# Block-sparse attention and a SoLU layer: where the first batch's mask factors are made, and how the weights and the first x come in

## The chip, the core and the metric

The kernel runs on one core of a Trainium2 chip. A core has five engines with an in-order queue each: TensorE (PE in the profile; PEld is its weight load), VectorE (DVE), ScalarE (ACT), GpSimd (POOL) and SyncE (SP), which here only issues DMAs. Data lie in SBUF, matmuls write to PSUM, and POOL works on SBUF alone. The metric is the device time of one execution in microseconds (us). The kernel before took 225.47 us, the median of three runs (225.02 to 226.38).

## The reference

Four batches, eight heads, 768 positions, head size 64. Positions are in 24 blocks of 32. A query block sees its neighbours, the first and the last block, three sampled key blocks, and the first and last query blocks see all. Then comes a layer of two weight matrices with SoLU (h times its softmax) and a layer norm with a gain between them.

```python
scores = scale * np.matmul(q, k.transpose(0, 1, 3, 2))
mask = np.abs(blk_i - blk_j) <= 1
mask = mask | (blk_i == 0) | (blk_j == 0) | (blk_i == 23) | (blk_j == 23)
for qb in range(24):
    for kb in sampled_blocks[qb]:
        mask[qb*32:(qb+1)*32, kb*32:(kb+1)*32] = True
attn = softmax(np.where(mask, scores, -1e9))
x = np.matmul(attn, v)                      # -> (3072, 512): all heads side by side
h = x @ w_in                                # w_in 512 x 1024
solu = h * softmax(h)
ln = (solu - mean(solu)) / sqrt(var(solu) + 1e-6) * g_ln
out = ln @ w_out                            # w_out 1024 x 512
```

## The kernel before, in words

**The mask as 24 more rows.** The masked scores come out of one matmul with 88 contraction rows: 64 of the head, and 24 in which KT holds which block a key belongs to (`selT`, one row per block) and QT holds -30000 or 0 for each pair of query and key block. KT and QT are `[128, heads x 6 chunks, 128]` in bf16, two of each, for alternating batches. The 24 rows depend on neither batch nor head, so they are written once into each of the two buffers (`mask_rows`, L595, which copies 24 x 1536 for two heads at a time).

**From k and q to KT and QT.** `load` (L302) brings k, q or v of a pair of heads as fp32 (position = 6 times partition plus chunk), `cast` (L317) makes bf16 in `kn`, `qn` (two heads side by side, 128 columns) or `VA` (v with a column of ones), `turn_mm` (L326) transposes a chunk of both heads on PE into PSUM, and `turn_out` (L339) copies the two halves of 64 rows to the two heads' places. In the first batch DVE copies straight from PSUM; later DVE copies the bank once to `pt` and POOL copies the halves.

**Units.** Twelve passes (batch and two of six query chunks) have twelve slots each (four head pairs, three units of key chunks): slot s has four score matmuls (`scores`, L363, into one of two `sco` buffers of PSUM), one exponential of 128 x 1024 on ACT (`exps`, L377) and eight matmuls of 65 columns (`outs`, L385, into the one `op` bank). After a pair's third unit `normalise` (L401) divides on DVE and so frees `op`. After a pass `x_turn` (L417) transposes x with a DMA, and the following pass's slots carry its two token tiles: `h_mms` (L422, into the one `h` buffer), `e_exp`, `solu` (DVE reads `h` last), `ln_turn` (DMA), `stats` and `rstd`, `o_mms` (L482, into the one bank `o`), `scaled`, `store`. The transposes of k and q from the second batch on use the bank `o` too.

**The order is written by hand.** `at(when, fn, ...)` (L290) puts a step into a plan; `emit` sorts it by `when`, counted in slots, and every engine gets its instructions in that order. A step's `when` is therefore no time, only a place in each engine's queue. What stands before slot 0 is issued in the order of the code. `zeros` (L557) are matmuls of zeros that keep PE busy at the start.

**The weights.** w_in (fp32 in memory) comes in one DMA from the POOL queue that casts on the way (L654). w_out comes in four DMAs on SP into a buffer of its own; `prep_w` (L665) multiplies it by g on POOL, `prep_mean` takes its column mean by matmuls, and `prep_cen` (L681) subtracts that on DVE in eight instructions, so that the layer norm's mean needs no work later.

In the first pass `outs` run late by `lag` slots (L706), because v is cast after k and q.

## Time and profile before

| | |
|---|---|
| median of 3 runs | 225.47 us |
| the profiled execution itself | 226.19 us |
| its span, first to last instruction | 224.5 us |
| PE busy, mean granted clock | 208.4 us (93%), 0.99 |
| ACT, DVE, POOL busy | 175.0, 155.7, 110.5 us |
| first exponential (slot 0) starts | 7.82 us |
| exponentials of slots 4, 9, 12, 18 start | 12.43, 20.00, 24.39, 30.20 us |
| `e_exp` of the first token tiles | 34.45, 43.47, 53.26 us |

The span runs from the first to the last instruction; the execution's own time has 1.7 us more around it. From 80 to 200 us PE is busy for 97 to 99% of the time, so a microsecond that PE loses before that comes back nowhere. The stretch from 0 to 70 us holds all that the change touches. In the timeline's rows the columns are start, duration, engine, line and operation, what is written and read with shape and type, how many instructions are merged, and in brackets the idle time of the engine just before, with what ended it. A matmul's duration includes its way through the array; how fast matmuls follow one another is read from their starts.

### The profile page before, as it was taken

Reading aid. Unit: us, or ns where it says so; the run is one execution under the profiler, and the core shown is the slowest. Engines: PE = TensorE matmul, PEld = TensorE weight load, DVE = VectorE, ACT = ScalarE, POOL = GpSimd, SP = SyncE. Lnnn points to the kernel's source line nnn. Section 1 sums busy time; section 2 is a strip of 40 time slices with the busy share of each in tenths; the row PEclk is TensorE's granted clock in tenths of the full one; section 3 lists DMA queues with packets and bytes.
Section 4 is the critical chain, followed back from the end, with each engine's and each line's share of the span. In section 5 each row is a group of like instructions: output and inputs, shape, how many; then the busy total and the mean of one; then the engine's idle time right before and its main releaser. Section 6 shows DMA issues by size and latency. Waiting matters only on the chain.

```text
span 224.5 us, 5886 instructions
## 1 busy us (share of the span) xinstructions
PE 208.4 (93%) x2328; PEld 146.2 (65%) x2367; DVE 155.7 (69%) x354; ACT 175.0 (78%) x204; POOL 110.5 (49%) x152
## 2 busy tenths in 40 slices
PE   7997998889969999999999999999999999999992
PEld 2576875666737667668667766767766766666451
DVE  7894865986785756856865766777775576566782
ACT  4885888677765988986978988887898898877471
POOL 7999985437874333494862525646840000000000
PEclk9996999999999999999999999999999999999999
DMA  6999595249998239979729749659731552434404
GB/s 199 379 362 289 114 280 165 47 27 303 283 231 262 60 85 175 287 128 257 214 47 230 241 90 288 175 38 289 198 72 36 140 78 62 100 93 110 117 0 149
DMA packets 56149, 37.59 MB, mean 167 GB/s; under 512 B 38069, under 2 KB 51637, under 8 KB 56117
## 3 DMA queue, kind: packets, MB, share of 16 engines
q1 hardware_dynamic: 55172, 35.60, 61.4%
q0 software_dynamic: 528, 1.05, 2.5%
q10 hardware_dynamic: 416, 0.52, 0.7%
q8 instruction: 19, 0.31, 0.6%
q14 instruction: 14, 0.11, 0.2%
HBM read 23.07 MB, written 6.29 MB: 131 GB/s over the span
## 4 chain that ended last, share of the span: by engine, by line
PE 69%; POOL 8%; DVE 8%; DMA 7%; ACT 2%; issue 2%; SPq 0%; POOLq 0%; DVEq 0%; ACTq 0%
PE sco L370 24%; PE op L394 14%; PE h L427 13%; PE o L487 13%; DMA xT<-xb 7%; POOL VA L315 2%; PE tp_q L335 2%; DVE stats L462 2%; PE he L801 2%; DVE w_cen_sb L682 1%; PE tp_k L335 1%; ACT exs L381 1%; POOL kn L315 1%; POOL qn L315 1%; DVE xb L408 1%
## 5 line engine op out<-in xcount | busy, mean ns | idle before, releaser
L381 ACT ACTIVATE exs<-sco 128x1024 bf16<-128x1024 f32 x144 | 142.0, 1025 | 17.9 <-PE sco L370 15.1
L370 PE MATMUL sco<-QT,KT 88*128 88x256 bf16 x576 | 87.6, 274 | 2.0 <-ACT exs L381 1.2
L370 PEld LDWEIGHTS <-KT 88*128 88x128 bf16 x576 | 55.1, 97 | 33.3 <-issue 6.2
L394 PE MATMUL op<-VA,exs 128*128 128x65 bf16 x1152 | 52.7, 195 | 1.9 <-POOL qn L315 1.6
L394 PEld LDWEIGHTS <-exs 128*128 128x128 bf16 x1152 | 49.4, 98 | 5.6 <-issue 2.3
L427 PE MATMUL h<-w_in_sb,xT 128*128 128x512 bf16 x153 | 49.5, 378 | 3.6 <-DMA xT<-xb 2.7
L480 POOL TENSOR_TENSOR rstd<-vpe,mhalf 128x1 f32<-128x1 f32 x24 | 13.5, 561 | 70.9 <-DVE vpe L478 65.4
L487 PE MATMUL o<-w_cen_sb,lnT 128*128 128x512 bf16 x162 | 43.5, 379 | 2.1 <-DVE pt_q L344 1.4
L436 ACT ACTIVATE e<-h 128x1024 bf16<-128x1024 f32 x22 | 22.5, 1024 | 19.2 <-PE h L427 14.9
L462 DVE BATCH_NORM_STATS2 stats<-solu 128x6 f32<-128x512 bf16 x48 | 30.6, 680 | 0.0
L315 POOL COPY KT<-pt_k 64x768 bf16<-64x768 bf16 x24 | 20.0, 835 | 20.6 <-DVE pt_k L344 20.0
L407 DVE RECIPROCAL recip_all<-op 128x4 f32<-128x4 f32 x48 | 8.7, 181 | 30.6 <-PE op L394 30.2
L448 DVE TENSOR_TENSOR solu<-h,e 128x1024 bf16<-128x1024 f32 x22 | 26.7, 1215 | 1.2 <-ACT e L436 1.2
L487 PEld LDWEIGHTS <-lnT 128*128 128x128 bf16 x176 | 15.8, 97 | 15.0 <-issue 1.5
L315 POOL COPY QT<-pt_q 64x768 bf16<-64x768 bf16 x24 | 20.1, 836 | 6.9 <-DVE pt_q L344 5.5
L498 DVE TENSOR_SCALAR ot<-o,rstd 128x512 f32<-128x512 f32 x20 | 15.0, 750 | 11.0 <-issue 7.4
L408 DVE TENSOR_TENSOR xb<-op,recip_all 128x256 bf16<-128x256 f32 x48 | 20.4, 424 | 1.7
L427 PEld LDWEIGHTS <-xT 128*128 128x128 bf16 x176 | 15.6, 98 | 7.6 <-DMA xT<-xb 3.7
L315 POOL CAST qn<-st_q 128x768 bf16<-128x768 f32 (+2 forms) x19 | 13.4, 711 | 4.1 <-DMA st_q<-in_q_dram 3.7
L315 POOL CAST kn<-st_k 128x768 bf16<-128x768 f32 x15 | 12.8, 851 | 3.6 <-DMA st_k<-in_k_dram 2.0
L344 DVE COPY pt_q<-tp_q 128x768 bf16<-128x768 bf16 x12 | 6.7, 556 | 10.0 <-PE tp_q L335 10.0
L315 POOL CAST VA<-st_v 128x768 bf16<-128x768 f32 x13 | 11.6, 911 | 0.9 <-DMA st_v<-in_v_dram 0.6
(82 smaller groups left out, 152.1 us busy)
## 6 DMA issues: line engine op xcount, KB each, us to landing
st_v<-in_v_dram SPq DMA_DIRECT2D x16, 384.0 KB, 5.8
out_dram<-ot SPq DMA_DIRECT2D x23, 256.0 KB, 3.7
st_k<-in_k_dram SPq DMA_DIRECT2D x15, 384.0 KB, 4.8
st_q<-in_q_dram SPq DMA_DIRECT2D x12, 384.0 KB, 5.1
w_out_f<-in_moe_w_out_dram SPq DMA_DIRECT2D x4, 512.0 KB, 6.6
st_q<-in_q_dram SPq DMA_DIRECT2D x4, 256.0 KB, 6.6
w_in_sb<-in_moe_w_in_dram POOLq DMA_DIRECT2D x1, 1024.0 KB, 12.6
st_q<-in_q_dram SPq DMA_DIRECT2D x4, 128.0 KB, 3.8
```

The costliest lines, as they stand in the source:

```text
L315: eng.tensor_copy(out=o, in_=i)
L370: nc.tensor.matmul(sco[:, hh, kk * QW : (kk + 1) * QW], KT[b % 2][0:KR, h * NCH + 2 * u + kk, :], QT[b % 2][0:KR, h * NCH + PC * j : h * N ...
L381: nc.scalar.activation(out=exs_of[ps, pr][:, u].rearrange("p a b c -> p (a b c)"), in_=sco_of.pop(s).rearrange("p a b -> p (a b)"), func=A ...
L394: nc.tensor.matmul(op[:, hh, ic, :], exs[:, u, hh, kk, ic * TQ : (ic + 1) * TQ], VA[b % 2][:, 2 * pr + hh, 2 * u + kk, :], start=(u == 0 a ...
L408: nc.vector.tensor_tensor(out=xb_of[ps][:, :, 2 * pr * D : 2 * (pr + 1) * D].rearrange("p c (h d) -> p h c d", h=2), in0=op[:, :, :, 0:D], ...
L427: nc.tensor.matmul(h_of[ps, i][:, half, :], xT_of[ps][:, i * KD + c, :], w_in_sb[:, c, half * HF : (half + 1) * HF], start=(c == 0), stop= ...
L436: nc.scalar.activation(out=o, in_=h, func=ACT.Exp, scale=1.0, accum_out=esum_all[:, t : t + 1])
L448: nc.vector.tensor_mul(out=so, in0=h, in1=e)
L462: nc.vector.bn_stats(out=stat_of[ps, i][:, half, :], in_=so[:, half, :])
L480: nc.gpsimd.tensor_tensor(out=rstd_of[ps, i], in0=vpe, in1=mhalf, op=ALU.pow)
L487: nc.tensor.matmul(ops_of[ps, i], lnT_of[ps, i][:, c, :], w_cen_sb[:, c, :], start=(c == 0), stop=(c == KF - 1), skip_group_check=True)
L498: nc.vector.tensor_scalar(out=o, in0=i_, scalar1=r, scalar2=None, op0=ALU.mult)
```

## The change

In the first batch `kn` and `qn` get 88 columns per head, 64 of the head and 24 of the mask's factors, and each head's chunk is transposed by itself, so that the 24 rows arrive in KT[0] and QT[0] together with the head's. The factors in natural form are `oh` (made on POOL) for k, and `m_sb` for q, from six small matmuls; `mask_cols` copies them in, one copy for each head: two on POOL for the first pair's k, two on DVE for the first two chunks of the first pair's q, and then fourteen on POOL, twelve for q and k of the other pairs and two for the rest of the first q. The second buffers, KT[1] and QT[1], still get their rows by copies, one on POOL and seven on DVE. w_in and w_out come as sixteen uncast pieces of 128 x 512 on SP in buffers shared with the late q chunks, and POOL casts w_in. The first x is transposed on PE (`x_first`) and copied by DVE. The second batch's loads, casts and transposes, the column mean, and the first tile's `o` stand at other places in the plan.

```diff
+    kn = fix.tile([TQ, NP, NCH * 2 * KR], BF16, name="kn")
+    qn = fix.tile([TQ, NP, NCH * 2 * KR], BF16, name="qn")
...
+    def natural(b, pr, key):
+        t = (kn if key == "k" else qn)[:, pr]
+        if b == 0:
+            return t.rearrange("p (c h r) -> p c h r", h=2, r=KR)
+        return t[:, 0 : NCH * 2 * D].rearrange("p (c h r) -> p c h r", h=2, r=D)
...
-                       bufs={NCH: 7, 2: 4, 4: 4}[c1 - c0])
+                       bufs={NCH: 7, 2: 4, 4: 9}[c1 - c0])
...
+        src = natural(b, pr, key)
+        tp = bank(pool, f"tp_{key}{b}_{pr}_{c0}")
         turned[key, b, pr, c0] = tp
-
-    def turn_out(b, pr, key, engs, c0=0, c1=NCH):
+        if b == 0:
+            for hh in range(2):
+                for c in range(c0, c1):
+                    o = (tp[0:KR, hh, (c - c0) * TQ : (c - c0 + 1) * TQ] if pool in (p_h, p_sco)
+                         else tp[0:KR, hh * 512 + (c - c0) * TQ : hh * 512 + (c - c0 + 1) * TQ])
+                    nc.tensor.matmul(o, src[:, c, hh, :], ident, is_transpose=True,
+                                     start=(c == c0), stop=(c == c1 - 1))
+            return
+        for c in range(NCH):
+            nc.tensor.matmul(tp[:, c * TQ : (c + 1) * TQ],
+                             src[:, c].rearrange("p h d -> p (h d)"), ident,
+                             is_transpose=True, start=(c == 0), stop=(c == NCH - 1))
+
+    def turn_out(b, pr, key, eng, c0=0, c1=NCH):
...
+            w = (c1 - c0) * TQ
+            i = tp if len(tp.shape) == 3 else tp.rearrange("p (h x) -> p h x", h=2)
+            o = dst[0:KR].rearrange("p (h c) t -> p h (c t)", c=NCH)[
+                :, 2 * pr : 2 * pr + 2, c0 * TQ : c1 * TQ]
+            if w > 512:
+                for hh in range(2):
+                    copy(eng, o[:, hh], i[0:KR, hh, 0:w])
+            else:
+                copy(eng, o, i[0:KR, :, 0:w])
+            return
+        pt = a_sm.tile([128, S], BF16, tag="pt", name=f"pt_{key}{b}_{pr}")
+        nc.vector.tensor_copy(out=pt, in_=tp[:, 0:S])
         for hh in range(2):
             h = 2 * pr + hh
-            copy(engs[hh], dst[0:D, h * NCH + c0 : h * NCH + c1, :],
-                 tp[hh * D : (hh + 1) * D, c0 * TQ : c1 * TQ].rearrange("p (c t) -> p c t", t=TQ))
+            copy(nc.gpsimd, dst[0:D, h * NCH : (h + 1) * NCH, :],
+                 pt[hh * D : (hh + 1) * D, :].rearrange("p (c t) -> p c t", t=TQ))
...
+    def x_first(ps):
+        xT_of[ps] = mo_sb.tile([128, PC * KD, 128], BF16, tag="xT", name=f"xT{ps}")
+        tp = bank(p_o, "x_tp")
+        xb = xb_of.pop(ps).rearrange("p c m -> p (c m)")
+        for c in range(PC * KD):
+            nc.tensor.matmul(tp[:, c * 128 : (c + 1) * 128], xb[:, c * 128 : (c + 1) * 128], ident,
+                             is_transpose=True, start=(c == 0), stop=(c == PC * KD - 1))
+        nc.vector.tensor_copy(out=xT_of[ps].rearrange("p c t -> p (c t)"), in_=tp)
...
+            nc.gpsimd.affine_select(out=oh, in_=oh, compare_op=ALU.is_ge, fill=0.0,
+                                    base=base, channel_multiplier=NCH * sg,
+                                    pattern=[[sg, NCH], [-BLK * sg, NB]])
+
+        def mask_cols(eng, key, pr, m, c0=0, c1=NCH):
+            for hh in range(2):
+                copy(eng, natural(0, pr, key)[:, c0:c1, hh, D:KR], m[:, c0:c1, :])
+
+        mask_cols(nc.gpsimd, "k", 0, oh)
...
-        zeros(8)
-
+        zeros(3)
+        oh_t = bank(p_h, "oh_t")[:, 0]
+        for c in range(NCH):
+            nc.tensor.matmul(oh_t[0:NB, c * TQ : (c + 1) * TQ], oh[:, c, :], ident,
+                             is_transpose=True, start=(c == 0), stop=(c == NCH - 1))
+        selT = fix.tile([NB, NCH, TQ], BF16, name="selT")
+        zeros(3)
+
+        dist = fix.tile([NB, NB], FP32, name="dist")
+        nc.scalar.activation(out=dist, in_=io_f[:, 1], func=ACT.Square, scale=1.0)
+        nc.scalar.activation(out=seen[:, NR], in_=dist, func=ACT.Relu, scale=-0.5, bias=1.0)
+        nc.scalar.copy(out=selT.rearrange("p c t -> p (c t)"), in_=oh_t[0:NB, 0:S])
...
+        for r in range(NR):
+            nc.vector.tensor_scalar(out=seen[:, r], in0=io_f[:, 0], scalar1=samp_f[:, r : r + 1],
+                                    scalar2=None, op0=ALU.is_equal)
+        any_f = fix.tile([NB, NB], FP32, name="any_f")
+        nc.vector.reduce_max(out=any_f, in_=seen.rearrange("p r k -> p k r"), axis=AX.X)
+        mask_l = fix.tile([NB, NB], BF16, name="mask_l")
+        nc.vector.tensor_scalar(out=mask_l, in0=any_f, scalar1=0.25, scalar2=neg_r,
+                                op0=ALU.is_lt, op1=ALU.mult)
...
+        m_ps = p_sco.tile([128, 2, 512], FP32, tag="sco", name="m_ps")[:, 0, 0 : NCH * NB].rearrange(
+            "p (c r) -> p c r", c=NCH)
+        for c in range(NCH):
+            nc.tensor.matmul(m_ps[:, c, :], selT[:, c, :], mask_l, start=(c == 0),
+                             stop=(c == NCH - 1), skip_group_check=True)
+        m_sb = fix.tile([TQ, NCH, NB], BF16, name="m_sb")
+        mask_cols(nc.vector, "q", 0, m_ps, 0, 2)
+        nc.vector.tensor_copy(out=m_sb, in_=m_ps)
+        for pr in range(1, NP):
+            mask_cols(nc.gpsimd, "q", pr, m_sb)
+            mask_cols(nc.gpsimd, "k", pr, oh)
+        mask_cols(nc.gpsimd, "q", 0, m_sb, 2, NCH)
...
+        turn_out(0, 0, "k", nc.vector, 0, 2)
+        turn_mm(0, 0, "q", p_op, 0, 2)
+        turn_out(0, 0, "q", nc.scalar, 0, 2)
+        zeros(1)
+        turn_mm(0, 0, "k", p_sco, 2, NCH)
+        turn_out(0, 0, "k", nc.vector, 2, NCH)
+        zeros(1)
+        scores(0)
+        zeros(2)
+        scores(1)
+        cast(nc.gpsimd, 0, 1, "k", 0, 2, 0)
+        cast(nc.gpsimd, 0, 1, "q", 0, 2)
+        cast(nc.gpsimd, 0, 1, "k", 2, NCH, 0)
+        turn_mm(0, 1, "k", p_h, 0, 2)
+        turn_out(0, 1, "k", nc.vector, 0, 2)
+        turn_mm(0, 1, "q", p_op, 0, 2)
+        turn_out(0, 1, "q", nc.vector, 0, 2)
+        turn(0.85, 0, 1, "k", p_o, 2, NCH)
...
-            at(w0 - 1.0, mask_rows, nc.vector, KT[0], 2 * pr)
-            at(w0 - 0.99, mask_rows, nc.vector, QT[0], 2 * pr)
             turn(w0, 0, pr, "k", p_h)
             turn(w0 + (0.05 if pr == 2 else 1.0), 0, pr, "q", p_o, 0, 2)
-        for pr in range(NP):
-            at(2.0 + 0.1 * pr, cast, nc.gpsimd, 0, pr, "v")
-            at(5.0 + 0.1 * pr, cast, nc.gpsimd, 0, pr, "q", 2, NCH)
-        for pr, when in enumerate((8.9, 10.4, 12.9, 14.9)):
+        V, G = nc.vector, nc.gpsimd
+        for eng, when, t, t0, h0 in (
+            (G, 2.05, KT[1], KT[0], 0), (V, 6.9, KT[1], KT[0], 2), (V, 7.6, KT[1], KT[0], 4),
+            (V, 9.0, KT[1], KT[0], 6), (V, 16.4, QT[1], QT[0], 0), (V, 18.3, QT[1], QT[0], 2),
+            (V, 20.3, QT[1], QT[0], 4), (V, 30.4, QT[1], QT[0], 6),
+        ):
+            at(when, mask_rows, eng, t, t0, h0)
+        for n, (key, pr) in enumerate((("v", 0), ("v", 1), ("v", 2), ("q", 0), ("v", 3),
+                                       ("q", 1), ("q", 2), ("q", 3))):
+            at(2.0 + 0.1 * n, cast, nc.gpsimd, 0, pr, key, *(() if key == "v" else (2, NCH)))
+        for pr, when in enumerate((9.4, 11.9, 13.4, 15.4)):
             turn(when, 0, pr, "q", p_o, 2, NCH, later=0.06)
         at(4.5, nc.gpsimd.memset, mean_w, 1.0 / d_ff)
         at(4.5, nc.gpsimd.memset, ones_c, 1.0)
         at(4.5, nc.gpsimd.memset, mhalf, -0.5)
-        for n in range(4):
-            at(n + 0.9, zeros, 3, p_op)
-
-        def w_load_in():
-            nc.gpsimd.dma_start(out=w_in_sb, in_=moe_w_in.rearrange("(c p) f -> p c f", p=128))
-
-        def w_load_out(n0, n1):
-            if n0 == 0:
+        for n in range(5):
+            at(n + 0.9, zeros, 2, p_op)
...
+        def w_load(which, c, half=0):
+            if which == "g":
                 nc.sync.dma_start(out=g_ln_sb, in_=moe_g_ln.rearrange("(c p) -> p c", p=128))
-            for n in range(n0, n1, 2):
-                nc.sync.dma_start(
-                    out=w_out_f[:, n : n + 2, :],
-                    in_=moe_w_out.rearrange("(c p) d -> p c d", p=128)[:, n : n + 2, :])
+                return
+            src = moe_w_in if which == "in" else moe_w_out
+            w_st[which, c, half] = a_st.tile([128, HF], FP32, tag="st4", name=f"w_{which}{c}_{half}",
+                                             bufs=9)
+            nc.sync.dma_start(
+                out=w_st[which, c, half],
+                in_=src[c * 128 : (c + 1) * 128, half * HF : (half + 1) * HF])
+
+        def prep_in(c, half):
+            nc.gpsimd.tensor_copy(out=w_in_sb[:, c, half * HF : (half + 1) * HF],
+                                  in_=w_st["in", c, half])
...
-        def prep_cen(c):
-            nc.vector.tensor_sub(out=w_cen_sb[:, c, :], in0=w_out_sb[:, c, :], in1=mean_sb)
-
-        at(2.25, w_load_in)
-        at(9.0, w_load_out, 0, 6)
-        at(12.1, w_load_out, 6, KF)
-        for n in range(H):
-            t, h0 = (KT[1], QT[1])[n % 2], 2 * (n // 2)
-            if n < 5:
-                at(7.0 + 0.1 * n, mask_rows, nc.gpsimd, t, h0)
-            else:
-                at(13.1 + 1.5 * (n - 5), mask_rows, nc.vector, t, h0)
+        def prep_cen(c0, c1):
+            nc.vector.tensor_sub(
+                out=w_cen_sb[:, c0:c1, :], in0=w_out_sb[:, c0:c1, :],
+                in1=mean_sb.rearrange("p (o d) -> p o d", o=1).broadcast_to([128, c1 - c0, d_model]))
+
+        for half in range(2):
+            for c in range(KD):
+                at(0.2, w_load, "in", c, half)
+                at(12.0, prep_in, c, half)
+        at(0.2, w_load, "g", 0)
         for c in range(KF):
-            at(13.0 + 0.1 * c, prep_w, c)
-            at(23.1 + 0.45 * c, prep_cen, c)
-        for n in range(4):
-            at(19.85 + n, prep_mean, 2 * n, 2 * n + 2)
+            at(0.2, w_load, "out", c)
+            at(13.0, prep_w, c)
+        at(22.85, prep_mean, 0, 4)
+        at(23.85, prep_mean, 4, 8)
+        at(25.3, prep_cen, 0, 4)
+        at(26.5, prep_cen, 4, 8)
...
-            lag = max(0, 3 - pr) if ps == 0 else 0
+            lag = 4 - pr if ps == 0 else 0
...
+        b1_load = [17.0, 17.4, 17.8, 18.2, 24.0, 24.4, 24.9, 27.3, 27.9, 28.5, 29.1, 29.7]
+        b1_cast = [23.2, 24.3, 25.3, 26.5, 30.6, 31.8, 33.0, 34.2, 35.4, 38.6, 40.2, 43.2]
+        for (key, pr), t_l, t_c in zip(ld, b1_load, b1_cast):
+            at(t_l, load, nc.sync, srcs[key], 1, pr, key)
+            at(t_c, cast, nc.vector if key == "v" and pr > 0 else nc.gpsimd, 1, pr, key)
+        for (key, pr), when in zip(kq, (25.9, 27.2, 30.4, 31.4, 34.9, 36.4, 37.6, 40.9)):
+            turn(when, 1, pr, key, p_o, later=0.08)
...
-            at(b0 - 0.1, x_turn, ps)
+            at(b0 + (0.95 if ps == 0 else -0.1), x_first if ps == 0 else x_turn, ps)
...
-                os = hs + (12 if ps == LP - 2 and i == PC - 1 else 14)
+                os = hs + {(0, 0): 16, (LP - 2, 1): 12}.get((ps, i), 14)
```

## The prediction

> **What bounds the kernel now.** I read the page's slices first: from 80 us on PE is 97 to 99% busy, so the end is set by the matmuls plus whatever PE loses earlier. So I looked at how much each engine does in each microsecond of the start, then at DVE's and PE's rows in time, and last at SP's queue.
>
> Stretches of one microsecond (columns: stretch, length, busy time and instructions of PE, PEld, DVE, ACT, POOL, granted clock, DMA share, GB/s):
>
> ```profile
> 16.00:17.00 1.00, 0.65 (x10) 0.34 (x6) 0.97 (x3) 1.00 (x2) 1.00 (x4) 1.00 1.06 381
> 17.00:18.00 1.00, 0.00 (x0) 0.00 (x0) 0.93 (x3) 0.82 (x1) 1.00 (x3) 1.00 1.07 385
> 18.00:19.00 1.00, 0.72 (x17) 0.74 (x18) 0.61 (x3) 0.00 (x0) 0.94 (x3) 0.83 1.10 272
> 19.00:20.00 1.00, 1.00 (x11) 0.77 (x9) 0.00 (x0) 0.00 (x1) 1.00 (x1) 0.50 1.07 256
> 20.00:21.00 1.00, 1.00 (x11) 0.59 (x8) 0.59 (x2) 1.00 (x1) 0.96 (x2) 0.50 1.11 270
> 21.00:22.00 1.00, 1.00 (x17) 0.87 (x17) 0.01 (x1) 0.80 (x2) 0.96 (x2) 0.50 1.09 268
> ```
>
> PE stands still for about 1.7 us, and then runs at half its clock for some 3.3 us. DVE's rows show why:
>
> ```profile
> 14.12 1.11 DVE L596 COPY KT<-selT 24x1536 bf16<-24x1536 bf16 x1
> 15.24 1.08 DVE L596 COPY QT<-QT 24x1536 bf16<-24x1536 bf16 x1
> 16.34 1.12 DVE L315 COPY KT<-tp_k 64x768 bf16<-64x768 bf16 x2
> 17.49 0.18 DVE L407 RECIPROCAL recip_all<-op 128x4 f32<-128x4 f32 x1
> 17.71 0.42 DVE L408 TENSOR_TENSOR xb<-op,recip_all 128x256 bf16<-128x256 f32 x1
> ```
>
> Mask rows stand before the division that frees `op`; it ends at 18.13. PE's row names POOL, but POOL's casts of v had ended, and the freed `op` fits the time:
>
> ```profile
> 18.28 0.77 PE L394 MATMUL op<-VA,exs 128*128 128x65 bf16 x16 [1.62 <-POOL qn L315]
> ...
> 45.49 1.67 PE L487 MATMUL o<-w_cen_sb,lnT 128*128 128x512 bf16 x6 [1.36 <-DVE pt_q L344]
> ...
> 67.20 0.61 PE L427 MATMUL h<-w_in_sb,xT 128*128 128x512 bf16 x2 [2.15 <-DMA xT<-xb]
> ```
>
> The second wait is DVE again, behind eight `w_cen_sb` instructions; the third is a DMA transpose issued at 59.48 right behind bulk loads, which lands after 7.67 us (median 2.8):
>
> ```profile
> 58.50 0.38 SPq L306 DMA_DIRECT2D st_v<-in_v_dram  x1
> 59.48 1.50 SPq L419 DMA_TRANSPOSE xT<-xb  x1
> ```
>
> **The change, step by step.** All times are of the profiled execution, 226.19 us around a span of 224.5; it lies 0.72 above the median of 225.47, which I take off at the end.
>
> **1. Up to slot 4: -1.8.** The mask path gets shorter, but q's columns need `m_sb`: three compares at 0.23 and two small operations end at about 4.1 on DVE; on PE six zeros at 0.45 (eight took 3.59), six turns and six small matmuls end at about 5.3; three small DVE copies, of about 0.2 each by the 64x256 row's 0.29, give `m_sb` at 6.0. The first exponential starts at 7.4 (now 7.82). All fourteen POOL copies stand behind `m_sb` and ahead of pair 1's casts. POOL takes 0.40 for 256 elements and 0.82 for 768 (starts 0.35 and 0.77 apart), so 144 elements take 0.26: 3.55 us, until 9.6, and the casts of k and q for the first two chunks until 10.3. Behind POOL's wait for `m_sb` stand all its casts, and behind PE's wait for these casts the rest of its queue: PE's queue has pair 1's turns before slot 2's scores, so that exponential moves from 9.8 to 11.2. Then 8 and 12 turns at 0.058 (six in 0.35), four zeros and four turns hold slots 3 and 4: slot 4 at 14.2, now 12.43. Bounds: -0.8 (0.20 a copy, as for the 24x24 selects) and -2.8 (0.31 and DVE in the way: the 0.82 cast has taken 1.21).
>
> **2. Slots 4 to 12: +2.1.** This stretch takes 11.96 now. Eight exponentials 0.935 apart (as from 24.39 on) are 7.5. To that I add 1.0 for slots in which scores (0.43), two `outs` (0.5) and 12 turns (0.7) exceed 0.935, and 1.4 for DVE: after slot 6's `outs` it has a division (0.64), two mask copies (0.95 each, mean of the contended ones), a division, a third copy and the copy of the first q's rest (0.153 + 1024 x 0.000525 = 0.69, from 64x512 and 64x768), 4.8 us in all, and slot 12's scores wait for the last of them. With the scores and the hand-overs (0.75) exponential 12 starts 5.6 after those `outs`, where ACT alone would have it at 4.2. Sum 9.9. Eight mask copies are gone from DVE (5.1 us of the seven until 16.3), so the stall and the slow clock go. Bounds: +0.4 and +4.4 (nothing but exponentials).
>
> **3. x on TensorE: -2.5.** `x_first` stands right behind slot 11's `outs` and its division. From the end of slot 14's scores: `outs` 0.26, division and hand-over 0.87, eight turns 0.63 to their end, DVE's copy 0.69 + 0.1, then the turns of q (the same bank `o`) 0.46 and slot 15's scores 0.43: 3.4 us, and 0.2 until ACT has them, while two exponentials cover 1.9: 1.7. Slot 14's scores are 0.55 late already, by eight turns ahead of them, and slots 16 to 18, with their turns and the first `h`, hold PE for another 0.7 beyond the exponentials. The present wait for xT at 29.06 (PE 0.23, its queue 0.5) goes: 1.7 + 0.55 + 0.7 - 0.45. Queued behind the waiting turns on PE are q's turns, slot 15's scores and slot 12's `outs`; ACT waits for the scores. Between slots 12 and 18 there is no slack to take it up: they take 5.81 now, six exponentials 5.6. Bounds: -3.2 and -1.5.
>
> **4. The column mean, -0.5.** Its matmuls fill PE now while slot 20.5's `e_exp` keeps the scores waiting (idle 0.99 at 36.53). Two pairs (0.86) move to where PE is full. Bounds -1.0 and 0.
>
> **5. DVE in slots 24 to 28, -1.5.** After the mean: 0.69, division 0.64, rstd 0.8, `w_cen` four at a time (0.15 + 2048 x 0.000525 = 1.2), pt 0.55, 1.2 again, division 0.64, `solu` 1.21: 6.9 us until `h` is free. PE has 4.2 of work in its queue up to the next `h`, ACT 4.6 for two exponentials and `e_exp`. PE loses about 2.8 there, against 1.36 now. Bounds -2.5 and +1.4 (the present wait goes, no new one comes).
>
> **6. Bank `o` at slots 30.4 and 31.4, -1.6.** The turn of k stands two matmuls (0.43) behind the last `o`, and waits for division and scaling (0.64 + 0.75): 0.9. The next turn waits for rstd 0.8, mask rows 0.9 and pt 0.55: 0.7 to 1.0. Bounds -2.0 and 0.
>
> **7. The third x: +2.2.** All twelve loads now stand before slot 30; the DMA transpose of slot 35.9 has no load right in front, lands in 2.8 and is needed four slots later. Bounds 0 and 2.5.
>
> **At nothing:** `lag` makes `outs` one slot later, but pair 0's exponentials are read by slot 6.8 and their buffer is needed again at slot 9; of the zeros two go, which are filler; the copy of the first q on ACT (0.6) lies in the wait for the scores. And the weights. SP issues seventeen small loads (0.45 each, 8 us); the late ones wait for buffers that POOL's casts free, the last until about 25.5, and the second batch's first loads stand behind them: about 26, now 28.27, needed at slot 23.2. POOL loses selects and row copies of 12 us and the DMA's 0.97 and gains 11, so it comes to `prep_w` at 26, now 26.40. The last v load waits for a buffer that a cast of slot 30.6 frees; behind it SP has a store and the DMA transpose of slot 33, 2.4 slots later. If that cover went, the mean and the second batch's casts would be as late as POOL.
>
> Sum: -1.8 + 2.1 - 2.5 - 0.5 - 1.5 - 1.6 + 2.2 = -3.6, hence 229.8, and **229.1** against the median.
>
> **Rivals.** **DVE never binds (222.3, 0.27).** Its queue is the cause in steps 2, 5 and 6. For it: uncontended mask copies took 0.55, and the change takes 5.1 us of them out of the first 16. Then step 2 is +4.4, step 5 +1.4 and step 6 zero, 6.8 better in all. It decides at whether the third KT copy is done before slot 12's scores are due, 3.75 us after slot 6's `outs`. Against it: POOL casts throughout, and copies beside it took 0.72 to 1.11. **It binds half the time (225.7, 0.18).** **The clock drops again (232.3, 0.10).** PE idles 1.9 us before pair 1's turns and 1.7 around `x_first`; now 1.7 us cost half clock, and slots 9 to 12 took 4.39 instead of 2.8: 1.6 each time, twice 3.2. Against it: the 2.15 us before 67.2 left the clock at 1.00. The Trainium skill, page "TensorE: Matmul & The Clock Gate", Part 1, says that the clock halves after an idle free-running window of about 3.4 us, and Part 4 that transposes don't count as busy in the same way; the slow stretch here has that length, but came after half as long an idle time. **Narrow weights load slower (231.3, 0.07).** 96 turns now load 88 columns; a load lasts 97 ns in the rows, hidden at a spacing of 58. With all of it bare they would be 39 ns apart more, 3.7 us; about 60% lies where PE binds, 2.2. No row shows 88 columns at full clock. The same page, "Weight-path perf modes", gives the fast load only to weights of 128 columns, and by its 73 ns the extra would be 96 x 15 ns, an estimated 1.4 us.
>
> **The numbers.** The forecast alone (227.7 to 231.2) has 0.38. Slower by over 1%, about what can be told here, is that with the last two, 0.55; within 1% 0.18; faster 0.27. The range leaves about 0.08 below, where DVE's rival and the shorter POOL copies meet, and 0.07 above: 221.8 to 233.0.
>
> **What would show it.** Step 1: fourteen POOL copies of about 0.26 from 6.0 and the third exponential at 11.2. Step 2: exponential 12 at about 24, with scores behind DVE. Step 3: ACT idle over 2 us before exponential 15. Steps 5 and 6: PE waiting on `solu`, `ot` and `pt` between its second and third `e_exp`. Step 7: no wait of `h` for xT. I would be wrong first if exponential 12 starts before 22.5, or if PE has no idle time beyond 1.4 us in slots 24 to 32.

## The result and the profile after

The changed kernel takes **232.1 us** (median of six executions, 230.46 to 232.5) beside 225.25 for the kernel before: **1.027 times** as long, 95% interval 1.024 to 1.031. The forecast was 229.1 us, slower, in a range of 221.8 to 233.0: the sign and the range held, the size was too small. The median lies 6.85 us above before's, where 3.6 were forecast. (Ratios and intervals here and below leave out executions in a slower state, more than 1.5% above the fastest of their kernel.)

The six executions are not alike: 230.46 and 231.1, and four from 232.08 to 232.5. The profiled one is the fastest, with a mean granted clock of 0.996; those at 232 have 0.989 to 0.993. So two things have to be explained: 4.27 us between the two profiled executions (230.46 against 226.19), and another 1.64 from there to the median. (The last 0.94 is that before's profiled execution was above its own median of 225.25.)

The page of the changed kernel, its span and the engines' busy time:

```profile
span 228.9 us, 6063 instructions
...
PE 211.5 (92%) x2428; PEld 148.4 (65%) x2428; DVE 148.8 (65%) x343; ACT 174.9 (76%) x206; POOL 108.3 (47%) x166
```

DVE has 6.9 us less to do than before, and yet the span is 4.4 longer. PE is 3.1 busier, since the first batch's turns are now one per head, 48 more at about 0.06, and eight of x came; the 3.1 is no exact price, because before's profiled execution had 3.4 us at half clock and its trace lacks some matmul records. Now the starts of the exponentials, by which the steps were forecast (timeline of ACT; start, duration, and in brackets the idle time before with what ended it):

```profile
10.97 1.02 ACT L409 ACTIVATE exs<-sco 128x1024 bf16<-128x1024 f32 x1 [1.67 <-PE sco L398]
...
14.05 2.85 ACT L409 ACTIVATE exs<-sco 128x1024 bf16<-128x1024 f32 x3 [0.74 <-PE sco L398]
...
24.16 1.94 ACT L409 ACTIVATE exs<-sco 128x1024 bf16<-128x1024 f32 x2 [1.30 <-PE sco L398]
...
30.08 6.21 ACT L409 ACTIVATE exs<-sco 128x1024 bf16<-128x1024 f32 x6 [2.31 <-PE sco L398]
36.85 1.02 ACT L473 ACTIVATE e<-h 128x1024 bf16<-128x1024 f32 x1 [0.57 <-PE h L464]
```

They are slots 2, 4, 12 and 15, and the first `e_exp`. Slot 4 is late by 1.62, slot 12 early by 0.23, and the first `e_exp` (34.45 before) late by 2.40. The kernel gains a stretch in the middle and loses on both sides of it.

PE's rows with idle time, from the timeline of the changed kernel:

```profile
9.73 0.42 PE L350 MATMUL tp_k<-ident,kn 128*88 128x128 bf16 x4 [1.53 <-POOL kn L321]
...
23.46 0.61 PE L398 MATMUL sco<-QT,KT 88*128 88x256 bf16 x4 [0.81 <-DVE QT L321]
...
28.93 0.61 PE L350 MATMUL tp_q<-ident,qn 128*88 128x128 bf16 x8 [0.78 <-DVE xT L457]
...
47.68 0.51 PE L354 MATMUL tp_q<-ident,qn 128*128 128x128 bf16 x6 [0.61 <-POOL qn L321]
...
50.44 0.59 PE L464 MATMUL h<-w_in_sb,xT 128*128 128x512 bf16 x2 [1.69 <-DVE solu L485]
...
55.79 0.50 PE L354 MATMUL tp_k<-ident,kn 128*128 128x128 bf16 x6 [0.74 <-DVE ot L535]
...
66.86 0.49 PE L354 MATMUL tp_k<-ident,kn 128*128 128x128 bf16 x6 [0.64 <-DVE pt_q L373]
...
76.61 0.38 PE L398 MATMUL sco<-QT,KT 88*128 88x256 bf16 x2 [0.87 <-POOL QT L321]
```

The three waits of before (1.62, 1.36 and 2.15) are gone, and eight others stand in their place; a ninth, for ACT behind the first `e_exp`, was 0.99 and is 1.43 (at 38.93). The wait for `solu` at 50.44 was in no row of before; what it waited for stands in DVE's rows:

```profile
45.21 1.22 DVE L741 TENSOR_TENSOR w_cen_sb<-w_out_sb,mean_sb 128x2048 bf16<-128x2048 bf16 x1
46.42 0.56 DVE L373 COPY pt_k<-tp_k 128x768 bf16<-128x768 bf16 x1
46.89 1.81 DVE L741 TENSOR_TENSOR w_cen_sb<-w_out_sb,mean_sb 128x2048 bf16<-128x2048 bf16 x1
...
49.18 1.21 DVE L485 TENSOR_TENSOR solu<-h,e 128x1024 bf16<-128x1024 f32 x1
```

DVE is busy without a gap from 43.62 to past 50; `solu`, which frees `h`, comes after all the centring.

### The profile page after: what moved, and what is told of

It is laid out like the page before. It is cut to its first block, busy times and chain, and to the rows that moved or that the text cites. A ratio compares the mean times of both kernels' runs of the same rounds, so it can differ in the third digit from the quotient of the medians.

```text
span 228.9 us, 6063 instructions
## 1 busy us (share of the span) xinstructions
PE 211.5 (92%) x2428; PEld 148.4 (65%) x2428; DVE 148.8 (65%) x343; ACT 174.9 (76%) x206; POOL 108.3 (47%) x166
## 5 line engine op out<-in xcount | busy, mean ns | idle before, releaser
L398 PE MATMUL sco<-QT,KT 88*128 88x256 bf16 x576 | 86.7, 272 | 3.3 <-ACT exs L409 1.6
L464 PE MATMUL h<-w_in_sb,xT 128*128 128x512 bf16 x176 | 55.2, 378 | 1.7 <-DVE solu L485 1.7
L517 POOL TENSOR_TENSOR rstd<-vpe,mhalf 128x1 f32<-128x1 f32 x24 | 14.3, 596 | 83.8 <-DVE vpe L515 78.5
L422 PE MATMUL op<-VA,exs 128*128 128x65 bf16 x1152 | 52.0, 194 | 1.5 <-DVE xb L436 0.9
L422 PEld LDWEIGHTS <-exs 128*128 128x128 bf16 x1152 | 48.7, 97 | 5.2 <-PE sco L398 1.3
L524 PE MATMUL o<-w_cen_sb,lnT 128*128 128x512 bf16 x176 | 45.1, 379 | 0.0
L321 POOL CAST kn<-st_k 128x768 bf16<-128x768 f32 (+2 forms) x16 | 13.5, 846 | 3.3 <-DMA st_k<-in_k_dram 3.1
L321 POOL CAST VA<-st_v 128x768 bf16<-128x768 f32 x13 | 10.5, 825 | 1.8 <-DMA st_v<-in_v_dram 1.7
```

What stands on the lines that cost most here:

```text
L321: eng.tensor_copy(out=o, in_=i)
L398: nc.tensor.matmul(sco[:, hh, kk * QW : (kk + 1) * QW], KT[b % 2][0:KR, h * NCH + 2 * u + kk, :], QT[b % 2][0:KR, h * NCH + PC * j : h * N ...
L422: nc.tensor.matmul(op[:, hh, ic, :], exs[:, u, hh, kk, ic * TQ : (ic + 1) * TQ], VA[b % 2][:, 2 * pr + hh, 2 * u + kk, :], start=(u == 0 a ...
L464: nc.tensor.matmul(h_of[ps, i][:, half, :], xT_of[ps][:, i * KD + c, :], w_in_sb[:, c, half * HF : (half + 1) * HF], start=(c == 0), stop= ...
L517: nc.gpsimd.tensor_tensor(out=rstd_of[ps, i], in0=vpe, in1=mhalf, op=ALU.pow)
L524: nc.tensor.matmul(ops_of[ps, i], lnT_of[ps, i][:, c, :], w_cen_sb[:, c, :], start=(c == 0), stop=(c == KF - 1), skip_group_check=True)
```

## The experiments

Each kernel ran beside the kernel before on its chip (medians there 226.46, 226.03 and 225.53, in three groups of runs). Where an edit is of the changed kernel, its effect is read at the `e_exp` of the token tiles, which start at 36.85, 46.08, 59.08, 68.55 and 77.75 in the changed kernel and at 34.45, 43.47, 53.26, 62.15 and 72.92 before. I call them E1 to E5. Each is of one profiled execution; the changed kernel profiled a second time (the control below) has E1 and E2 within 0.02 of the first.

**POOL's order at the start (step 1).**

```diff
         for pr in range(1, NP):
-            mask_cols(nc.gpsimd, "q", pr, m_sb)
             mask_cols(nc.gpsimd, "k", pr, oh)
-        mask_cols(nc.gpsimd, "q", 0, m_sb, 2, NCH)
+        mask_cols(nc.gpsimd, "q", 1, m_sb)
...
         cast(nc.gpsimd, 0, 1, "k", 2, NCH, 0)
+        mask_cols(nc.gpsimd, "q", 2, m_sb)
+        mask_cols(nc.gpsimd, "q", 3, m_sb)
+        mask_cols(nc.gpsimd, "q", 0, m_sb, 2, NCH)
```

> The changed kernel with only GpSimd's order changed: k's mask columns of all pairs are copied while GpSimd waits for the q factors, then q's columns of pair 1 and pair 1's casts, and the other eight copies after those. Same work. Theory: pair 1's casts end about 2.5 us earlier, exponential 2 starts at about 9.3 instead of 10.97, slot 4 at about 12.5 instead of 14.05, and the end comes about 1.5 us earlier: 230.6. Theory with the clock beside it (most executions of the changed kernel lose another 1.6 us because TensorE's 1.7 us of idle time lowers its clock): 3.1 us earlier, 229.0, and the runs lie closer together. Rival (vector-engine copies of mask rows set slot 12 whatever comes before): under 0.5 us.

Measured: 228.55 to 230.05 in three executions and 232.78, at a mean clock of 0.981, in a fourth; ratio 1.020 (1.009 to 1.031). So the runs did not move closer together. Before and after the edit, POOL's rows (changed kernel first, then this one):

```profile
5.86 0.56 POOL L321 COPY qn<-m_sb 128x144 bf16<-128x144 bf16 x2 [2.77 <-DVE m_sb L648]
...
8.85 0.48 POOL L321 COPY qn<-m_sb 128x96 bf16<-128x96 bf16 x2
9.28 0.40 POOL L321 CAST kn<-st_k 128x256 bf16<-128x256 f32 x1
```

```profile
2.55 2.04 POOL L321 COPY kn<-oh 128x144 bf16<-128x144 bf16 x8
5.87 0.56 POOL L321 COPY qn<-m_sb 128x144 bf16<-128x144 bf16 x2 [1.28 <-DVE m_sb L648]
6.57 0.40 POOL L321 CAST kn<-st_k 128x256 bf16<-128x256 f32 x1
```

Pair 1's first cast starts at 6.57 and not at 9.28, the first three exponentials run without a gap from 7.47, slot 4 starts at 12.32, and all five `e_exp` come 1.90 earlier. So what slot 4 lost lay in the order of POOL's queue. The copies did not get cheaper: they were put where POOL stood idle (2.77) or where nobody waited.

**DVE's three copies into KT[1] (step 2).**

```diff
-            (V, 6.9, KT[1], KT[0], 2), (V, 7.6, KT[1], KT[0], 4),
-            (V, 9.0, KT[1], KT[0], 6),
+            (V, 15.6, KT[1], KT[0], 2), (V, 17.2, KT[1], KT[0], 4),
+            (V, 19.2, KT[1], KT[0], 6),
```

> The changed kernel, with the three copies of mask rows into KT[1] that stand on DVE at 6.9, 7.6 and 9.0 slots put at 15.6, 17.2 and 19.2 (they are read from slot 36 on). Theory (step 2): at 21.94 the third of them lasts 0.74 and stands right ahead of the copy of the first q's rest, for which slot 12's scores wait 0.81 on PE. Without it exponential 12 starts 0.6 to 0.9 earlier than 24.16, the wait of PE for QT goes, and the first e_exp and the end come 0.6 to 0.9 earlier, unless the copies in slots 15 to 19 hold up something there. Rival (DVE does not bind): exponential 12 and the end move by less than 0.3.

Measured: median 229.82 (229.27 to 230.92), ratio 1.018 (1.012 to 1.024). The wait for QT at 23.46 is gone, and where the changed kernel had exponentials 10 and 11, a gap of 1.30, and then 12 and 13, the four now run without a gap:

```profile
20.73 4.19 ACT L409 ACTIVATE exs<-sco 128x1024 bf16<-128x1024 f32 x4 [0.24 <-PE sco L398]
```

E1 is 1.18 earlier and E5 1.17: a little more than expected. DVE did bind there.

**The first x in another bank, two slots later (step 3).**

```diff
-        tp = bank(p_o, "x_tp")
+        tp = bank(p_h, "x_tp")[:, 0]
...
-            at(b0 + (0.95 if ps == 0 else -0.1), x_first if ps == 0 else x_turn, ps)
+            at(b0 + (2.95 if ps == 0 else -0.1), x_first if ps == 0 else x_turn, ps)
```

> The changed kernel with the first x turned two slots later (after slot 16's scores instead of behind slot 11's division) and into the idle bank of h instead of bank o; all work is still done. Theory (TensorE's in-order waits add up to the end): the 2.31 us that ScalarE idles before exponential 15 go, exponential 15 starts about 27.8 instead of 30.1, and the end comes 1.7 to 2.2 us earlier, so about 230.1 against 232.1. Rival (the wait is only the visible end of a slower chain, and the next wait, on bank o or on the first h, takes its place): less than 0.5 us, 231.6 or more.

Measured: 229.69, 229.75, 231.33 and 231.38, ratio 1.018 (1.009 to 1.026). ACT's row at slot 15 is now

```profile
28.17 1.94 ACT L409 ACTIVATE exs<-sco 128x1024 bf16<-128x1024 f32 x2 [0.42 <-PE sco L398]
```

1.91 earlier; E1 and E2 are 1.30 earlier, where 1.7 to 2.2 were expected, most of the rest going to a new gap of 0.53. PE's wait of 0.78, in which the turns of q needed bank `o` and DVE still copied x out of it, is gone. The edit moves x to another bank and to a later place at once, so what each of the two gave is not told apart. The two pairs of times, with mean clocks of 1.0, 1.0, 0.993 and 0.993, are 1.6 apart; the profiled one of the slower pair ran at half clock from 49.28 to 52.70, right behind the waits of 0.61 and 1.69.

**Mean, centring, the first `o` and the second batch's first casts and turns where they were (steps 4 to 6).**

```diff
-        at(22.85, prep_mean, 0, 4)
-        at(23.85, prep_mean, 4, 8)
-        at(25.3, prep_cen, 0, 4)
-        at(26.5, prep_cen, 4, 8)
+        for c in range(KF):
+            at(23.1 + 0.45 * c, prep_cen, c)
+        for n in range(4):
+            at(19.85 + n, prep_mean, 2 * n, 2 * n + 2)
...
-        b1_cast = [23.2, 24.3, 25.3, 26.5, 30.6,
+        b1_cast = [20.2, 21.4, 22.6, 23.8, 30.6,
...
-        for (key, pr), when in zip(kq, (25.9, 27.2, 30.4, 31.4,
+        for (key, pr), when in zip(kq, (23.84, 25.84, 29.84, 31.84,
...
-                os = hs + {(0, 0): 16, (LP - 2, 1): 12}.get((ps, i), 14)
+                os = hs + {(LP - 2, 1): 12}.get((ps, i), 14)
```

> The changed kernel with the column mean, its subtraction in eight pieces, the first o, the second batch's first four casts and its first four turns at the places that they have in the kernel before. Theory: TensorE's idle times between its first and third e_exp (1.43, 0.61, 1.69, 0.74 and 0.23 us, 4.7 in all) become those of the kernel before (0.99 and 1.36, 2.4 in all), so the end comes about 2.3 us earlier: 229.8. Rival (the matmuls only change places, and what is taken away in one slot is waited for in the next): under 0.7 us, 231.4 or more.

Measured: **227.69**, ten executions within 227.50 and 227.92, ratio 1.011 (1.007 to 1.014). E1 is 0.45 later, E3 2.95 and E5 3.58 earlier; after 40 us PE has two waits above 0.3 left:

```profile
48.35 1.67 PE L524 MATMUL o<-w_cen_sb,lnT 128*128 128x512 bf16 x7 [1.37 <-DVE pt_q L373]
...
73.03 0.38 PE L398 MATMUL sco<-QT,KT 88*128 88x256 bf16 x2 [0.87 <-POOL QT L321]
```

2.3 was expected. From profiled execution to profiled execution it gains 2.8, from median to median 4.4 (not side by side: the kernel before had 225.25 beside the one and 226.46 beside the other). All ten have a mean clock of 0.996 or more: with the waits of slots 27 to 31 the executions at the lower clock went too.

**The loads alone (step 7).** The kernel before with the second batch's loads at the changed kernel's places.

```diff
+            b1_load = {2: (17.0, 17.4, 17.8, 18.2), 5: (28.5, 29.1),
+                       4: (24.0, 24.4, 24.9, 27.3, 27.9, 28.5)}
...
-                at(t0 + 3.2 + 0.9 * n + (0.5 if b == 1 and w == 6 else 0), load, nc.sync, src, b,
-                   pr, key)
+                at(t0 + 3.2 + 0.9 * n if b > 1 else b1_load[w][n] + (0.6 if w == 5 else 0),
+                   load, nc.sync, src, b, pr, key)
```

> The kernel before with one part of the change alone: the second batch's twelve loads at the changed kernel's places in the queue, all before slot 30. Theory: the third x's DMA transpose finds no loads in front, lands in about 3 instead of 7.67 us, the 2.15 us wait of h at 67.2 goes, and the end comes 2.0 to 2.2 us earlier than the kernel before: about 223.2 against 225.3. Rival (another transfer or a wait for a staging buffer takes the place): no difference, 225.

Measured: median 224.26 (eight within 223.42 and 224.40, two at 228.6), ratio 0.993 (0.989 to 0.997). The wait for the third x is gone, but

```profile
70.40 0.38 PE L370 MATMUL sco<-QT,KT 88*128 88x256 bf16 x2 [0.87 <-POOL QT L315]
```

stands behind it. From E4 to E5 it takes 9.49 where before took 10.77: 1.28 of the 2.15, where 2.0 to 2.2 were expected. The 0.87 is the same as in the changed kernel: POOL's copies of the last q turn are that late anyway, and the wait for x had covered them.

**The lower clock: a first try.** Zeros of 512 columns (0.22 each) into bank `o`, to fill the waits of 0.61 and 1.69.

```diff
+        at(27.15, zeros, 2, p_o)
+        at(27.87, zeros, 6, p_o)
```

> The changed kernel, with eight matmuls of zeros (0.22 each at full clock) into the bank o: two ahead of the second batch's first q turns (slot 27.15), six ahead of the first h of slot 27.9. They run while TensorE now waits 0.61 and 1.69. Theory (the lower clock comes from these idle stretches): no row changes its place by more than 0.3, but the executions with a mean clock of 0.993 become executions with 0.996 or more, the median falls from 232.1 to between 230.3 and 230.9, and the runs lie within 0.6 of each other. Rival (the lower clock has another origin, or another place): the median stays at 231.8 to 232.4 with runs at 230.5 and at 232.

Measured: 232.62, 234.17, 235.59 and 235.84, with mean clocks of 0.998, 0.992, 0.984 and 0.983. The edit failed: the six zeros need the bank that DVE's `pt_q` frees, and on DVE that copy stands behind `solu`, so they began after the wait they were to fill and lengthened it to 2.15 (from 1.69). The failure shows more than the plan would have. The profiled execution (235.84) drops to half clock twice; in the stretches of one microsecond the columns are busy time of PE, PEld, DVE, ACT and POOL, then the granted clock, DMA share and GB/s:

```profile
23.00:24.00 1.00, 0.73 (x13) 0.69 (x14) 0.21 (x1) 0.02 (x1) 1.00 (x2) 1.00 1.02 294
24.00:25.00 1.00, 0.61 (x11) 0.34 (x8) 0.61 (x2) 1.00 (x2) 1.00 (x3) 0.99 1.04 399
25.00:26.00 1.00, 1.00 (x18) 1.00 (x19) 0.00 (x0) 0.92 (x1) 1.00 (x3) 0.50 1.09 414
...
28.00:29.00 1.00, 0.58 (x8) 0.32 (x6) 0.61 (x2) 0.79 (x1) 0.86 (x2) 0.81 1.05 378
...
51.00:52.00 1.00, 0.00 (x0) 0.00 (x0) 1.00 (x3) 0.14 (x1) 0.94 (x2) 1.00 1.09 381
52.00:53.00 1.00, 0.89 (x3) 0.40 (x3) 1.00 (x3) 0.00 (x0) 0.94 (x2) 0.64 0.95 338
53.00:54.00 1.00, 1.00 (x3) 0.30 (x2) 0.25 (x1) 0.00 (x0) 0.94 (x3) 0.50 1.08 135
...
55.00:56.00 1.00, 1.00 (x8) 0.61 (x7) 0.00 (x0) 0.00 (x0) 0.00 (x0) 0.65 1.07 309
```

The slices inside a stretch show 0.50 and those outside 1.00; a slice at a clock c therefore held 2(1 - c) us of half clock. So the first stretch runs from 24.98 to 28.38, the second from 52.28 to 55.70: 3.4 us each, in which PE does 1.7 us less work. That is the step between the executions: 232.62, 234.17 (+1.55), 235.59 and 235.84 (+2.97 and +3.22).

**The same, done right, beside a control.** The changed kernel again, and the changed kernel with zeros ahead of what PE waits for, in banks that are free by then.

```diff
...
+        for when, n, pool in ((10.79, 3, p_h), (12.94, 1, p_h), (13.39, 3, p_h), (20.75, 5, p_o),
+                              (27.15, 8, p_o)):
+            at(when, fill, n, pool)
```

> The changed kernel itself once more, as the control beside the next run on the same chip. By the clock theory its executions fall into steps of 1.6: 230.5 without a stretch at half clock, 232.1 with one, 233.7 with two, and most have one. By the rival (a spread without steps) they lie evenly between 230.5 and 232.5.

> The changed kernel with matmuls of zeros that end before what TensorE waits for: three ahead of slot 12's scores, one ahead of the first x and three behind it (bank h), five ahead of the scores of slot 20.8, and eight ahead of the turns of slot 27.2 (bank o, which DVE has freed by then). Nothing that DVE, ACT or POOL does changes, and the idle time that is left on TensorE from slot 11 to 28 is under 0.8 at a time. Clock theory: the half-clock stretches go, the median comes to 230.3 to 230.9 and lies 1 to 1.6 below the control, its mean clock is 0.996 or more. Rival (the clock has another cause): the same spread and median as the control, or later by the zeros that do not fit, up to 0.8.

| | us (mean clock) of each execution, in order of time taken |
|---|---|
| control | 231.08 (1.0), 232.1 (0.988), 232.17 (0.993), 233.37 (0.981), 233.5 (0.981), 234.04 (0.980) |
| with zeros | 231.56 (1.0), 231.7 (1.0), 231.82 (1.0), 231.87 (0.998), 231.98 (0.999), 232.13 (0.997) |

The medians are 232.77 and 231.84. The control's times fall into three groups, whose means lie 1.05 and 1.5 apart (1.6 and 1.6 were expected, with most executions in the middle one, where there are two); with the waits filled the mean clock is 0.997 or more in every execution, and all lie within 0.57. The median came out higher than the 230.3 to 230.9 I expected: the zeros have a price of their own, E2 is 0.93 later than in the control (47.02 against 46.09), since the five ahead of slot 20.8 pushed `h` to wait 0.93 for the first `solu`. Five of the control's six executions have a mean clock of 0.993 or less and none of the six with zeros, side by side on one chip: that is the evidence that idle time of PE makes the drops. The gain of 0.9 in time is less sure, since the two rows of times overlap.

**The edits that helped, together.** First the three of steps 1, 3 and 4 to 6; then the KT[1] copies too.

> The three edits that each helped, together: x turned two slots later in another bank, k's mask columns ahead of q's with pair 1's casts between, and mean, centring, first o and the second batch's first casts and turns at the places before. Theory (they act at different places and add): from the changed kernel's profiled 230.46 the terms -1.3, -1.9 and -2.8 give 224.5, in all undisturbed runs alike, since no idle time of TensorE near 1.7 is left after slot 12; ratio to the kernel before about 0.996. Rival (one gain is taken up by the next wait, DVE's copies in slots 6 to 12 above all): 225.5 to 226.5, ratio above 1.0.

> The same three edits, and the three KT[1] copies on DVE at slots 15.6, 17.2 and 19.2 as well. Theory: another 0.6 to 0.9 earlier than the three edits, 223.6 to 223.9, ratio 0.992 to 0.994, so faster than the kernel before. Rival: the copies now stand between DVE's turns, division and x in slots 15 to 19, and return there what they gave: the same as the three edits within 0.3, or later.

Measured, near both expectations: 224.59 (224.24 to 226.61), ratio 0.996 (0.992 to 1.000), and **223.66** (223.35 to 223.90), ratio **0.990** (0.984 to 0.995). At E5 the four together are 7.62 earlier than the changed kernel; the single effects, 1.90, 1.17, 1.30 (read at E1 and E2, because that run's profiled execution lost clock behind them) and 3.58, add up to 7.95. They are for the most part separate losses at separate places. Against the kernel before, E1 is 1.50 earlier and E5 2.79.

**What DVE's order still cost.**

```diff
-            at(23.1 + 0.45 * c, prep_cen, c)
+            at(23.1 + 0.45 * c if c < 4 else 25.53 + 0.1 * c, prep_cen, c)
...
-            at(es + 1.7, stats, ps, i)
+            at(es + (2.6 if (ps, i) == (1, 1) else 1.7), stats, ps, i)
```

> The version with the four edits, and two changes of DVE's order: the copy of the second pair-0 turn (q) stands ahead of the last four centring instructions instead of behind three of them, and the statistics of slot 40.2 stand behind the copy of the last q turn. Theory (DVE's order sets both waits that are left after 40 us, 1.37 on pt_q before the first o and 0.87 on QT): the first becomes 0.2 or less, the second 0.3 to 0.4, the end 1.2 to 1.7 earlier, 222.0 to 222.5, ratio 0.982 to 0.986. Rival (other work is just as late): o then waits for the centring of its later chunks and QT for POOL, and the gain is below 0.6.

Measured: **223.31** (222.96 to 223.63), ratio **0.991** (0.988 to 0.994), beside 225.53 for the kernel before; 222.0 to 222.5 and 0.982 to 0.986 were expected, and against the four edits the ratio shows no gain. Both waits are gone (no row of PE between 36 and 80 us has more than 0.3 but one):

```profile
46.62 0.59 PE L464 MATMUL h<-w_in_sb,xT 128*128 128x512 bf16 x2 [1.40 <-DVE solu L485]
```

It took the first one's place, because DVE's sum is what it was. E3 is not earlier (52.24 against 52.09), E5 0.61 earlier: the half of the edit that only reordered a full DVE gave nothing, the half behind slot 40, where DVE had slack, gave what it promised (0.5 to 0.6). The rival, other work just as late, held for the first half.

## Why the prediction was right in sign and too small

Forecast and measurement between the two profiled executions, as the sum of all losses so far:

| up to | steps | forecast | measured | what the run that undid it gave back |
|---|---|---|---|---|
| slot 4 | 1 | 1.8 | 1.62 | 1.90 |
| slot 12 | 2 | -0.3 | -0.23 | 1.17 more, by moving three copies |
| E1 (slot 20.5) | 3 | 2.2 | 2.40 | 1.30 |
| E2 (slot 26.5) | 4 | 2.7 | 2.61 | |
| E3 (slot 32.5) | 5, 6 | 5.8 | 5.82 | 2.95 at E3, 3.58 at E5, for 4 to 6 |
| E5 (slot 44.5) | 7 | 3.6 | 4.83 | |
| end of the span | | 3.6 | 4.4 | |

**Steps 1 to 3 held in their mechanism.** The fourteen copies start 0.25 apart (0.26 forecast) from 5.86 on, and the third exponential starts at 10.97 (11.2). In step 2 slot 12 starts at 24.16 (about 24), with the scores waiting 0.81 for the copy of q behind DVE's mask rows; the rival in which DVE never binds fell here, as the run with the copies moved confirms, and the one in which it binds half the time fell with DVE's waits in steps 5 and 6. In step 3 ACT is idle for 2.31 ahead of slot 15 (over 2 forecast); the step cost 2.63 (2.5), of which the run that moved x gave back 1.30, so about half of it has no experiment behind it.

How the first 12 slots split between steps 1 and 2 hangs on one execution of the kernel before. In the run with the loads alone, whose code is the same up to slot 17, slot 4 starts at 13.22 instead of 12.43 (a mask copy of DVE takes 1.21 at 8.20, against 0.55) and slot 12 at 24.27: against that execution step 1 costs 0.83 and step 2 gains 0.94. E1 agrees (34.33 and 34.45). That execution has no half-clock stretch in these slots and still reaches slot 12 only 0.12 sooner, so that a slow clock was part of what step 2 saved is not shown.

**Step 4** was put at 0.5, and PE's wait for ACT behind E1 did grow from 0.99 to 1.43, but E2 is only 0.21 worse than E1: the two matmul pairs that moved still found room. Small, and inside its bounds.

**Steps 5 and 6** come to 3.2 together (3.1), but not by my account of them. PE waits 0.61 + 1.69 where I had 2.8, so 0.94 more than the 1.36 of before, where step 5 had 1.5; and 0.97 (0.74 and 0.23) at the bank, where step 6 had 1.6. The remaining 1.3 of the 3.2 is busy time of PE between E2 and E3: 9.73, against 8.43 in the run with the loads alone, whose code is before's there (before's own trace lacks an `h` and an `o` and shows 8.32). Eight turns and two score matmuls that had stood on the other side of the two markers are about 0.7 of it by their spacing; the rest I can't place. Of the waits, 0.61 is not DVE's alone: the cast of q stands behind `rstd` in POOL's queue, which takes 1.40 and waited for DVE's `vpe`. I had read that stretch as one of DVE alone.

**Step 7 is the term of the sum that failed**: +2.2 forecast, and 5.82 - 4.83 = 1.0 came. A wait of 0.64 for `pt_q` at 66.86 appeared between E3 and E4, which I had not priced, and behind the wait for x stood the wait of 0.87 for QT. The run with the loads alone shows the second in the kernel before: the transfer costs it 1.28 and not 2.15, since POOL's copies are late by 0.87 in any case. (They were late because DVE handed them the turn late: the 0.87 went when DVE's statistics were moved behind that copy.) I asked of this step whether a load stood in front of the transfer, and not what is late next.

**The clock is the largest part of what the median was missed by.** Measured 232.1 lies 3.0 above the forecast 229.1: 0.66 is the sum's (230.46 against 229.8), 0.72 is what I took off because before's profiled execution lay above its median, while the changed kernel's lay below its own, and 1.64 is from there to the median. The profiled execution of the changed kernel has no half clock before its last microseconds. The control's has one stretch (the slice at 50 shows 0.97, that at 54 shows 0.82: 50.94 to 54.36); its E2 agrees with the other within 0.01 and its E3 is 1.64 later. The mean clocks of the unprofiled executions fit one such stretch in most, two in some of the control's. It was a rival, with 1.6 each time and 0.10; the price was right, the chance far too low. That the median came out at 232.1, beside that rival's 232.3, is partly luck: the 232.3 counted two stretches. I placed it at the 1.9 idle before pair 1's turns and the 1.7 around the first x. The control has it at 51 instead, behind waits that the forecast itself contained, the 0.61 and 1.69 of step 5:

```profile
51.00:52.00 1.00, 1.00 (x11) 0.77 (x9) 1.00 (x2) 0.01 (x1) 0.94 (x3) 0.50 1.06 396
52.00:53.00 1.00, 1.00 (x16) 0.72 (x15) 0.06 (x1) 1.00 (x1) 0.94 (x2) 0.50 1.19 263
```

The changed kernel's first profiled execution had the same waits, with PE's rows from 9.7 to 50 us within 0.02 us (before that up to 0.5 apart), and kept its clock. What I had against it, a wait of 2.15 in before that left the clock alone, was one execution of a thing that comes by chance, and the fastest execution of the changed kernel is another.

**Narrow weights** were a rival with 0.07. Their loads are longer (groups of weight loads of the changed kernel: number of them, busy time, mean ns of one):

```profile
L398 PEld LDWEIGHTS <-KT 88*128 88x128 bf16 x576 | 54.6, 97 | 33.3 <-issue 6.8 <-DVE QT L321 0.9 <-POOL KT L321 0.2
...
L350 PEld LDWEIGHTS <-kn 128*88 128x88 bf16 x48 | 3.3, 120 | 2.2 <-POOL kn L321 1.8
```

120 ns for 88 columns and 97 for 128 (the 88 in the first row are the rows). Yet twelve such turns follow one another at about 0.06 us, so the price was near zero. The Trainium skill, page "TensorE: Matmul & The Clock Gate", section "Weight-path perf modes", gives the fast load to 128 columns only: by direction the rows agree. The 73 ns for 88 columns that I took from that page of the Trainium skill were 120 here, and the measurement decides.

What remains open: the change between E5 and the end (4.83 to 4.4), and how far the last tenths of each median belong to the chip.

## What to carry to other kernels

A transfer or copy that is moved forward costs what it pushes back in its own queue: ask of each instruction moved which queue it stands in, and who waits for the one right behind it. With POOL's, DVE's and the bank's order put right, the changed kernel is 1% faster than the one before. That its core pays is only in part shown: the loads alone, in the kernel before, already give 0.7%, and the intervals overlap (0.989 to 0.997 and 0.984 to 0.995). Between the profiled executions the version with four edits is 1.4 earlier at E1, where no load has had an effect yet (32.95 against 34.33), but only 0.6 at the end of the span (222.0 against 222.6). When a wait is to go, look first at what else would be late at that moment; when an engine's order is changed where it is full, the wait only changes its name.

## What had not been expected

**The clock drops on a grid.** In the execution that dropped twice, the half-clock stretches begin at 24.98 and 52.28, 27.30 us apart, and last 3.4: eight such lengths. The Trainium skill, page "TensorE: Matmul & The Clock Gate", Part 1, gives a free-running window of 4096 cycles at 1.2 GHz, 3413 ns; eight of them are 27.30, and the trace agrees. Three more traces fit as well: from the stretch in the middle to the drop behind the last matmuls it is 177.5 in the control (50.94 to 228.44, 52 lengths), 180.9 in the run with x later (49.28 to 230.18, 53) and 204.8 in the kernel before (18.66 to 223.46, 60). So whether a wait is punished depends on where it falls in the window, which differs between executions of one kernel. Counted back from its last drop (226.92), the changed kernel's first profiled execution has a border at 49.43, inside the wait of 1.69, and PE is busy for 2.13 and 2.41 us in the windows on its two sides; the control has the whole wait of 1.69 in one window, with 1.56:

```profile
46.02:49.43 3.41, 2.13 (x29) 1.65 (x27) 3.38 (x6) 3.35 (x5) 3.41 (x4) 1.00 1.10 192
49.43:52.85 3.42, 2.41 (x27) 1.57 (x27) 2.62 (x4) 1.53 (x2) 3.24 (x5) 1.00 1.05 295
```

```profile
47.53:50.94 3.41, 1.56 (x13) 1.02 (x14) 3.38 (x6) 2.42 (x3) 3.35 (x4) 1.00 0.82 237
```

That is how the same rows run once at full clock and once at half. The wait of 2.15 in the kernel before, which left the clock alone, was divided too, by a border at 66.45.

**A window need not be idle.** The Trainium skill's table of the two clock states, in the same Part 1, has the clock fall after an idle window. In the execution that dropped twice, the window ahead of 24.98 held PE busy for 2.05 us, 60% of it, and none of its waits reached 1 us; the window ahead of 52.28 held 1.24. Here the measurement decides: several short waits in one window can be enough. Where the limit lies stays open, and PE's busy time alone does not set it: in the same trace the windows that begin at 7.91 and 38.63 held 1.88 and 1.91, less than 2.05, and no drop followed them.
